# Products with zero weights between the score and sum products of an attention kernel

## The chip, the cores and the metric

The kernel runs on one core of a Trainium2 chip. The metric is the device time of one execution in microseconds (us). A core has a matrix engine (TensorE, PE in the profile, its weight loads PEld), a vector engine (DVE), an engine for exponentials and the like (ACT), a general engine (POOL) and an engine that issues transfers (SP). Each takes its own instructions in order; they wait for each other by semaphores. Matrix products are written to PSUM, which has 8 banks of 512 fp32 columns by 128 partitions.

## The reference, cut to what matters

Four layers, two kinds, on 2048 tokens of 512 features, 32 heads of 16:

```python
x = x + _A_ref(_layernorm(x), A_wq, A_wk, A_wv, A_wo, A_beta)
x = x + _B_ref(_layernorm(x), B_wqkv, B_wo)
x = x + _A_ref(_layernorm(x), A_wq, A_wk, A_wv, A_wo, A_beta)
x = x + _B_ref(_layernorm(x), B_wqkv, B_wo)

def _B_ref(x, wqkv, wo):
    q, k, v = ...
    scores = jnp.einsum('bhqd,bhkd->bhqk', q, k) * Dh ** (-0.5)
    p = _softmax(scores, axis=-1)
    o = jnp.einsum('bhqk,bhkd->bhqd', p, v)
    return (lambda x, *d: x.transpose(*d))(o, 0, 2, 1, 3).reshape(B, S, D) @ wo
```

Kind A attends causally within each of four segments of 512 tokens, and adds a memory that is read with phi(q) and updated with phi(k) and v from segment to segment, mixed by a gate per head. Kind B is plain attention over all 2048 tokens.

## The kernel before, in words

The program is laid out by a planner in Python: it appends operations to one list per engine and derives all waits from the buffers and PSUM banks that they read and write (`Sched.add`). There is no loop on the chip.

The work is cut into *units*. A unit takes three PSUM banks, each with the scores of 128 keys by 512 queries of one head (kind A: 512, 384 + 128 or 256 columns, what the causal mask leaves). Two sets of three banks (0 to 2, 3 to 5) alternate. `unit()` (L970) issues three score products, with 32 rows of features each, `ps<-qm,KB` or `ps<-qm,KA` in the profile, and one ACT instruction that writes the exponentials of all three banks, `pT<-ps` (L1023). In kind B a unit may also hold a fourth score product, into bank 7, whose exponential DVE works out in steps (`dx_chain`, L747). `pv_step()` (L1128), two units later (three in kind A), issues the products of the exponentials with the values, `ps<-pT,VB` or `ps<-pT,VA` (from DVE's exponentials `ps<-dxo,VB`). These are the sums: weights of 128 rows and 17 columns (16 values and a one for the denominator), added up in bank 6, at partition 0, 32, 64 or 96, by `r`, which counts the four strips of 32 feature rows, two heads to a strip. A *group* is four heads, one of each strip, with 512 queries and their keys: 64 banks for a whole group of kind B (some are split over the key segments), 12 for one of kind A. After a group's last sum DVE transposes bank 6 (L1083), and the next group's first sum waits for that.

The main loop, `attention()` (L1154), does for each unit, in this order: scores and exponentials; outside kind A and when enough units lie ahead, background work that uses PE; sums that are due; background work. Background work is a list of tasks in generator form, run by credits for PE and DVE: layer norms, the projections to q, k and v (`proj_fm`, `proj_tm`, L488 and L499: four products of 512 columns by 128 rows, issued two at a time, `ps<-xT,wA`, `ps<-wA,xT` and the same with `wB`), the memory of kind A (`task_mem`) and the output products (`task_out`, L664: four products at once, `ps<-woA,oT` or `ps<-woB,oT`). They all go to bank 7. So PE's queue has, per unit: scores, maybe projections, sums, maybe projections, and then the next scores. Every product goes through `mm` (L324), so all have line L325.

The names that the change touches: `self.cur`, the group whose sums are in progress, or None between groups; `started[0]`, true once the sums of the group's head at partition 0 have begun; `wB`, the projection weights of kind B, loaded once at the start; `self.step`, the number of units begun.

## Time and profile before

| | us |
|---|---|
| median of 3 runs | 2149.47 |
| lowest, highest | 2146.08, 2149.75 |
| the profiled execution | 2149.91 |
| its span, first to last instruction | 2148.0 |
| ACT busy in the span | 2008.6 |
| PE busy in the span | 1789.5 |
| DVE busy in the span | 1593.3 |
| mean granted TensorE clock | 0.694 of full |

PE's busy time counts a product from its start to the modelled end of its last column, with the way through the array; several products of different rows or columns of the array run side by side. The costliest groups of instructions are the exponentials of L1023 (1985.8 us), the scores of kind B (682.5), the sums from ACT's exponentials (664.8) and from DVE's (205.4). Transfers are small: 24.5 MB, and the DMA engines are all but idle after the first fifth.

### The profile page before, as it was taken

To read this page: it belongs to the slowest core of one execution; us is meant where nothing else is said; L and a number is where in the kernel's file an instruction comes from. 1 tells how busy PE (TensorE), PEld (TensorE's weight loads), DVE (VectorE), ACT (ScalarE), POOL (GpSimd) and SP (SyncE) were. 2 spreads that over 40 slices of the span, in tenths; PEclk is the share of its full clock that TensorE was granted. 3 is DMA by queue.
4 is the path that set the end of the run, shared out by engine and by line. 5 is a ranking of instruction groups with operands and counts; after the bars stand their busy time and mean duration, and the time that the engine had idled before them with its cause. 6 is when DMAs were issued, how large, how long until landed. Compare 5 with 4: busy or idle time off the path is not lost.

```text
span 2148.0 us, 30875 instructions
## 1 busy us (share of the span) xinstructions
PE 1789.5 (83%) x11634; PEld 414.1 (19%) x11634; DVE 1593.3 (74%) x2806; ACT 2008.6 (94%) x1618; POOL 407.0 (19%) x832
## 2 busy tenths in 40 slices
PE   7788888888788787787877888888888888888888
PEld 3222222211211212212222112221111111111111
DVE  6655665487658885688857975548799989988996
ACT  5788998999989999899998998889999999999997
POOL 3532433020150002400033102501100000000000
PEclk9889888756957968769866558785655565556555
DMA  4011000000000000000000001000000000000000
GB/s 138 16 25 21 20 14 13 6 1 13 8 1 11 1 13 9 11 11 1 15 11 6 1 3 19 11 11 1 11 1 1 1 11 1 1 1 11 1 1 11
DMA packets 67125, 24.54 MB, mean 11 GB/s; under 512 B 59808, under 2 KB 66464, under 8 KB 66976
## 3 DMA queue, kind: packets, MB, share of 16 engines
q1 hardware_dynamic: 66976, 22.57, 4.6%
q8 instruction: 91, 1.49, 0.3%
q14 instruction: 58, 0.48, 0.1%
HBM read 6.30 MB, written 2.10 MB: 4 GB/s over the span
## 4 chain that ended last, share of the span: by engine, by line
issue 39%; ACT 28%; PE 19%; DVE 9%; POOL 4%; DMA 1%; SPq 0%; POOLq 0%; ACTq 0%; DVEq 0%
ACT pT L1023 27%; PE ps L325 19%; POOL ob L1096 1%; POOL pT L1038 1%; POOL qm L941 1%; DVE tT L1083 1%; DVE VB L341 1%; DVE VA L341 1%; DVE dxt L732 1%; DMA xT<-xn 1%; DVE QB L341 0%; ACT amem L513 0%; DVE x L686 0%; DVE lnst L431 0%; DVE QA L341 0%
## 5 line engine op out<-in xcount | busy, mean ns | idle before, releaser
L1023 ACT ACTIVATE pT<-ps 128x1536 bf16<-128x1536 f32 (+2 forms) x1589 | 1985.8, 1439 | 111.1 <-PE ps L325 97.9
L325 PE MATMUL ps<-qm,KB 32*128 32x512 bf16 x4096 | 682.5, 524 | 235.3 <-ACT pT L1023 217.6
L325 PE MATMUL ps<-pT,VB 128*17 128x512 bf16 x3716 | 664.8, 515 | 23.7 <-DVE tT L1083 18.3
L1096 POOL TENSOR_TENSOR ob<-tT,rd 128x256 bf16<-128x256 f32 x128 | 99.8, 780 | 1207.5 <-DVE rd L1087 1168.3
L732 DVE TENSOR_SCALAR dxt<-ps 128x512 uint32<-128x512 f32 x380 | 261.0, 687 | 86.3 <-PE ps L325 80.3
L325 PEld LDWEIGHTS ps<-qm,KB 32*128 32x128 bf16 x4096 | 133.8, 96 | 762.9 <-ACT pT L1023 679.6
L1038 POOL TENSOR_SCALAR_AFFINE_SELECT pT<-pT 128x256 bf16<-128x256 bf16 (+2 forms) x512 | 210.2, 427 | 322.4 <-ACT pT L1023 313.1
L766 DVE SCALAR_TENSOR_TENSOR dxo<-dxt,dxz 128x1024 int16<-128x1024 uint16 (+1 forms) x203 | 235.1, 1158 | 4.6
L325 PEld LDWEIGHTS ps<-pT,VB 128*17 128x17 bf16 x3716 | 119.1, 90 | 520.3 <-issue 452.9
L325 PE MATMUL ps<-dxo,VB 128*17 128x512 bf16 x380 | 205.4, 541 | 0.4 <-DVE dxo L766 0.4
L325 PE MATMUL ps<-qm,KA 32*128 32x512 bf16 (+3 forms) x1024 | 127.5, 376 | 39.6 <-ACT pT L1023 31.8
L760 DVE TENSOR_TENSOR dxz<-dxz,dxo 128x1024 f16<-128x1024 f16 (+1 forms) x203 | 135.1, 666 | 4.3
L325 PE MATMUL ps<-pT,VA 128*17 128x512 bf16 (+3 forms) x1024 | 121.2, 378 | 18.5 <-DVE tT L1083 10.9
L756 DVE TENSOR_SCALAR dxo<-dxt 128x1024 f16<-128x1024 uint16 (+1 forms) x203 | 132.9, 655 | 2.2 <-PE ps L325 2.0
L764 DVE TENSOR_TENSOR dxz<-dxz,dxo 128x1024 f16<-128x1024 f16 (+1 forms) x203 | 131.8, 649 | 2.1
L1083 DVE STREAM_TRANSPOSE tT<-ps 128x512 f32<-128x512 f32 x112 | 79.7, 712 | 70.6 <-PE ps L325 70.4
L941 POOL TENSOR_SCALAR qm<-QB,par 128x512 bf16<-128x512 bf16 x102 | 81.6, 808 | 180.2 <-PE ps L325 179.9
L758 DVE TENSOR_SCALAR dxz<-dxo 128x1024 f16<-128x1024 f16 (+1 forms) x203 | 88.7, 437 | 6.8
L325 PE MATMUL ps<-xT,wB 128*128 128x512 bf16 x256 | 82.9, 433 | 9.2 <-DMA xT<-xn 2.5
L686 DVE TENSOR_TENSOR x<-x,ps 128x512 bf16<-128x512 bf16 x64 | 44.0, 688 | 60.2 <-PE ps L325 60.0
L762 DVE TENSOR_SCALAR dxz<-dxz 128x1024 f16<-128x1024 f16 (+1 forms) x203 | 83.7, 412 | 6.7
L325 PE MATMUL ps<-xT,wA 128*128 128x512 bf16 x256 | 78.6, 419 | 10.3 <-DVE QA L341 5.3
(89 smaller groups left out, 917.9 us busy)
## 6 DMA issues: line engine op xcount, KB each, us to landing
out_dram<-x SPq DMA_DIRECT2D x8, 256.0 KB, 2.1
x<-in_A_x_dram SPq DMA_DIRECT2D x3, 512.0 KB, 10.9
wB<-in_B_wqkv_dram SPq DMA_DIRECT2D x1, 1536.0 KB, 12.7
xT<-xn SPq DMA_TRANSPOSE x60, 2.5
x<-in_A_x_dram SPq DMA_DIRECT2D x4, 128.0 KB, 2.4
wA<-in_A_wk_dram SPq DMA_DIRECT2D x1, 512.0 KB, 4.4
wA<-in_A_wq_dram SPq DMA_DIRECT2D x1, 512.0 KB, 5.5
wA<-in_A_wv_dram SPq DMA_DIRECT2D x1, 512.0 KB, 6.3
```

Source lines behind the costliest of these rows:

```text
L325: self.sc.add("pe", lambda e: e.matmul(out, lhsT, rhs, start=start, stop=stop, skip_group_check=True), reads=reads, banks=[(bank, "w", all ...
L732: self.op("dve", lambda e: e.tensor_scalar(self.dxt[:, b, i, :], o, SCALE * LOG2E * 65536, 127.0 * 65536, op0=ALU.mult, op1=ALU.add), writ ...
L756: self.op("dve", lambda e: e.tensor_scalar(f, lo, 2.0 ** -16, None, op0=ALU.mult), reads=bt, writes=bo)
L758: self.op("dve", lambda e: e.tensor_scalar(z, f, EXP_C3, EXP_C2, op0=ALU.mult, op1=ALU.add), reads=bo, writes=bz)
L760: self.op("dve", lambda e: e.tensor_tensor(z, z, f, ALU.mult), reads=bo + bz, writes=bz)
L764: self.op("dve", lambda e: e.tensor_tensor(z, z, f, ALU.mult), reads=bo + bz, writes=bz)
L766: self.op("dve", lambda e: e.scalar_tensor_tensor(ob, hi, 128.0, z, op0=ALU.mult, op1=ALU.add), reads=bt + bz, writes=bo)
L941: self.op(eng, (lambda m, q, col: lambda e: e.tensor_scalar(m, q, col, 0.0, op0=ALU.mult, op1=ALU.add))(m, q, col), reads=[bq, self.b_par] ...
L1023: self.sc.add("act", (lambda dst, src: lambda e: e.activation(dst, src, ACT.Exp, scale=SCALE))(dst, src), writes=self.b_pT[slot * 3 + i:sl ...
L1038: self.op("pool", (lambda blk, pat: lambda e: e.affine_select(blk, blk, pattern=pat, compare_op=ALU.is_ge, fill=0.0, base=0, channel_multi ...
L1083: self.op("dve", lambda e: e.transpose(tT.rearrange("p a b -> p (a b)"), src), reads=bsrc, writes=[bt], bank=bk, alloc=al)
L1096: self.op("pool", lambda e: e.tensor_tensor(ob, tT[:, :, 0:16], rb, ALU.mult), reads=[bt, br], writes=[self.b_ob[oi][g.e]])
```

## The change

A function `keep_busy` is called at the end of each unit from the eleventh on. If a group's sums are in progress and have begun at partition 0, it adds products to bank 6 until the unit has 1024 columns of background products. Projections and output products add 512 each to that count (`bg_cols`), the memory's products and the fourth score product don't. The added products have a tile of zeros, 128 rows by 17 columns, as weights and 512 columns of `wB` as moving data, and add to partitions 0 to 16 of the running sums without starting or ending them, so the sums keep their values. A unit without projections gets two, a unit with at least one pair of projections or output products gets none, and a unit between groups gets none.

```diff
+    BUSY_COLS = 1024
...
+        self.zero = sb("zero", [P, 17], bf)
...
+    def keep_busy(self):
+        g = self.cur
+        while g is not None and g.started[0] and self.bg_cols < self.BUSY_COLS:
+            bank = self.banks[6]
+            self.mm(self.ps[0:17, bank.col0:bank.col0 + 512], self.zero[:, :], self.wB[:, 0, 0:512], False, False,
+                    [self.b_zero, self.b_wB[0]], bank, g.acc)
+            self.bg_cols += 512
...
+        pool(lambda e: e.memset(self.zero[:, :], 0.0), [self.b_zero])
...
         for ci in range(NCH):
             if ci == 2:
                 yield ["cont"], 2, 690
+            self.bg_cols += 512
             self.mm(o, w[:, ci, off + c * 128:off + (c + 1) * 128], self.xT[:, slot, ci, :], ci == 0, ci == NCH - 1,
                     [bw] + self.b_xT[slot], bank, al)
...
             for n, (a, c, ba) in enumerate(srcs):
+                self.bg_cols += 512
                 self.mm(o, a[:, ti * 128:(ti + 1) * 128], wo[:, c, :], n == 0, n == len(srcs) - 1, list(ba) + [bwo], bank, al)
...
-        self.step = 0
+        self.step = self.bg_cols = 0
...
             self.run_deferred(False)
             self.background(False if split else None)
+            if self.step > 10:
+                self.keep_busy()
+            self.bg_cols = 0
             n += 1
```

The same line stands in `proj_tm` as in `proj_fm`. `BUSY_COLS` is a constant of the class.

More of the change, by code (lines that the diff above doesn't have):

```diff
@@ L298, in alloc @@
         self.b_dxt = n2("dxt", 2, 2)
-        self.b_dxz = B("dxz")
+        self.b_dxz, self.b_zero = B("dxz"), B("zero")
         self.b_dxo = n1("dxo", self.NDX)
@@ L684, in task_out @@
             for n, (a, c, ba) in enumerate(srcs):
+                self.bg_cols += 512
                 self.mm(o, a[:, ti * 128:(ti + 1) * 128], wo[:, c, :], n == 0, n == len(srcs) - 1, list(ba) + [bwo], bank, al)
```

## The prediction

> **What bounds the kernel now.** I read the page first, for the engines' shares.

> ```profile
> PE 1789.5 (83%) x11634; PEld 414.1 (19%) x11634; DVE 1593.3 (74%) x2806; ACT 2008.6 (94%) x1618; POOL 407.0 (19%) x832
> ...
> ACT  5788998999989999899998998889999999999997
> ...
> PEclk9889888756957968769866558785655565556555
> ```

> ACT does the exponentials and is busy 2008.6 of 2148.0 us. So 139.4 us of ACT idle is all that any change outside ACT can win. In the last quarter ACT's digits are 9 although the TensorE clock is near half. Next, who ACT waits for:

> ```profile
> ACT pT L1023 <- PE ps L325: 97.9, 137, 4.2
> ACT pT L1023 <- POOL pT L1038: 8.4, 16, 1.2
> ACT xT L476 <- PE ps L329: 7.4, 1, 7.4
> ```

> Of it 97.9 us is score products that came late. Then stretches in which the trace's clock record holds one value (it has only 1.0 and 0.5, 826 and 1317 us in all):

> ```profile
> 1304.00:1362.00 58.00, 48.97 (x354) 13.68 (x351) 28.48 (x53) 51.74 (x49) 16.65 (x38) 1.00 0.03 6
> 1758.00:1942.00 184.00, 161.47 (x935) 28.77 (x932) 167.00 (x260) 183.43 (x137) 14.48 (x16) 0.50 0.00 1
> ```

> Columns: length; busy time (instructions) of PE, PEld, DVE, ACT, POOL; clock. At full clock there are 354 products in 58 us, at half 935 in 184 us with ACT idle for 0.57 us only. The clock alone costs nothing while a unit has no projections. Now single units in the timeline: a plain one at half clock, one with two projection products at full clock, and one with four output products at half clock. Columns: start, length, engine, line, what, count.

> ```profile
> 1503.15 0.61 PE L325 MATMUL ps<-qm,KB 32*128 32x512 bf16 x3 [0.20 <-ACT pT L1023]
> 1503.69 0.60 PE L325 MATMUL ps<-pT,VB 128*17 128x512 bf16 x3
> 1504.50 0.61 PE L325 MATMUL ps<-qm,KB 32*128 32x512 bf16 x3 [0.20 <-ACT pT L1023]
> ```

> ```profile
> 177.53 0.39 PE L325 MATMUL ps<-qm,KB 32*128 32x512 bf16 x3
> 177.85 0.60 PE L325 MATMUL ps<-wA,xT 128*128 128x512 bf16 x2
> 178.39 0.39 PE L325 MATMUL ps<-pT,VB 128*17 128x512 bf16 x3
> 178.71 0.39 PE L325 MATMUL ps<-qm,KA 32*128 32x512 bf16 x3
> ```

> ```profile
> 1255.56 0.61 PE L325 MATMUL ps<-qm,KB 32*128 32x512 bf16 x3
> 1256.11 1.89 PE L325 MATMUL ps<-woB,oT 128*128 128x512 bf16 x4
> 1257.92 0.60 PE L325 MATMUL ps<-pT,VB 128*17 128x512 bf16 x3
> 1258.46 0.61 PE L325 MATMUL ps<-qm,KB 32*128 32x512 bf16 x3
> 1259.17 1.45 ACT L1023 ACTIVATE pT<-ps 128x1536 bf16<-128x1536 f32 x1 [1.18 <-PE ps L325]
> ```

> Starts are to be read: the unit of ACT is 1.34 us (1503.15 to 1504.50). At half clock the scores take PE 0.54 us and the sums again 0.54, 1.08 of 1.34. At full clock each takes 0.32 and a pair of projections 0.54: 1.18 in all, which fits. A single product of 512 columns streams 0.22 us at full clock (two end in 0.60, one in 0.39) and 0.43 at half. Four output products at half clock make a unit of 2.90 us (1255.56 to 1258.46); ACT then stands 1.18 us. So the loss lies where projections meet the half clock.

> **What sets the clock.** I cut the timeline into steps of 3.41 us (every stretch of the clock record is a multiple of it) and took, from the starts, the share of each step in which at least one product streams. Of 243 steps at full clock, the 35 with a share under 0.43 were all followed by half clock and the 201 from 0.45 up all by full. Of 385 at half clock, one of the 325 under 0.76 was followed by full, 3 of the 18 from there to 0.80, and 32 of the 42 above. Taken by occupied cells or by the number of products no such edge shows. A plain unit streams 2 x 0.213 of 1.34 us, 0.32, at full clock and falls back; at half clock it streams 0.64 and doesn't rise.

> **The change, part by part.** Setup gains one memset of 17 columns on POOL, beside loads that end later: nothing. The order of all old instructions is unchanged on every engine. PE gains 2092 products in 1046 pairs, after 1046 of the 1492 units (a unit: a run of score products up to the next). 325 units have projections or output products and get none, 121 have no sum in progress and get none. 765 of the pairs follow units that now run at half clock. A pair waits for nothing new: wB was issued at 13.4 us and landed 12.7 us later, the first pair comes at some 51 us. Behind it in PE's queue stand the next unit's scores, for which ACT waits.

> A pair has the sums' shape (128 rows, 17 columns), streams 2 x 0.213 us at full clock, and I charge it 0.43 to 0.54 us by the projection pair. A unit with it is then 1.07 to 1.18 us of PE at full clock, under ACT's 1.34. At half clock it is 1.82 to 1.93 us, over it. It streams 0.64 of 1.34 us at full clock, over the 0.43 edge, so the clock should stay. Where the three sums leave out the first quarter of the columns, the pair's first product can run beside them and the share is 0.48, still over. At half clock it streams 1.71 of 1.93 us, 0.88, over 0.80: the clock should rise within one or two steps. So I expect nearly full clock all along.

> ACT's idle time now, sorted by unit and clock (25.4 us lie before the first unit and can't change):
> - 53 units with projections at half clock: 32.6 us, 0.615 each. At full clock 272 such units have 39.4 us, 0.145 each. Full clock gives 53 x 0.47 = 24.9 us back. Ends: 10 us, if half of it is DVE or transfers late at those places, and all 32.6.
> - 78 units of the first kind of layer (A, narrower exponentials) that get pairs, at half clock: 20.0 us, 0.256 each. Nearest is the A unit with two projections at full clock, 0.184: 5.6 us back. Ends: 0 and 78 x (0.256 - 0.088) = 13, by the 25 such units now at full clock.
> - 942 B units that get pairs: 15.1 us now, 13 ns each in the 686 at half clock. With a pair at full clock PE's load (1.07 to 1.18) is about theirs (1.08). Ends: 13 ns each, 3 us back, and 56 ns, the B unit with four projections at full clock, 38 us lost. I take 20 ns, nearest the first: 4 us lost.
> - Relapses. Where a group ends, a unit has no pair and PE waits for the transpose of bank 6; a step there streams about (0.43 + 1.54 x 0.85)/3.41 = 0.51, with a unit of share 0.48 near 0.45, at the edge. One relapse: about 2 to 2.5 units at 1.82 to 1.93 us, 0.5 to 0.6 over ACT's 1.34 each, less some 0.5 us by which scores are early: 0.9 us. Of 128 group ends I take 9: 8 us. Ends: 0 and one in two, 58 us.

> Sum: -24.9 - 5.6 + 4 + 8 = -18.5 us. Span 2148.0 - 18.5 = 2129.5. Its own execution was 2149.91, 1.9 us beside the span and 0.4 above the median of the three: **2131 us**.

> [...]

> **Rivals.**
> 1. Slower: relapses decide. With 24.9 + 5.6 - 4 = 26.5 us won, 30 relapses at 0.9 us eat it. At one in two group ends: 2149.9 - 26.5 + 58 = 2181 us. For it: pairs turn a harmless half clock into a PE-bound one, and 128 group ends offer the place. Against: PE, when late, has no gaps, and 0.88 is well over the edge.
> 2. Nothing changes (within 0.2%, 4.3 us, what a measurement of this kernel can tell from no change): ACT idles for DVE, transfers and POOL behind PE, or wins equal losses. For it: at full clock the same units still idle 39.4 us. Against: four to 0.615.
> 3. The gate doesn't count products with zero weights, or few columns: the clock stays, and 765 pairs cost 0.59 us each, 451 us: 2600 us. Against: the edge was the same for steps filled by score products, sums or projections.
> 4. More is won: every low end at once, 2149.9 - 32.6 - 13 - 3 = 2101 us, with the rest of the half-clock idle some 2095.

> **How the numbers follow.** Forecast 0.50 (2112 to 2145), rival 4 0.14, rival 2 0.10, rival 1 0.20, rival 3 0.06. Faster by over 0.2% is forecast and rival 4, 0.64; same 0.10; slower 0.26. The range, 2095 to 2165, takes in 4, 2 and rival 1 up to some 45 relapses; what it leaves out is the rest of rival 1 and rival 3.

> **What would show it.** Right: PEclk at 9 in nearly all slices, ACT's wait for PE near 75 us, four-product units of about 1.6 us, ACT still gapless in the last quarter. Wrong: a mean clock under 0.9; many half-clock steps behind group ends with ACT idle there; or ACT idle in B units far over 20 ns at full clock, which would mean that PE's 1.18 of 1.34 leaves too little to catch up.

## The result, and the profile after

The changed kernel takes 2141.78 us (median of 6 runs, 2139.26 to 2142.92) against 2149.68 us, a ratio of 0.9963 (95% interval 0.9953 to 0.9974): faster by 0.37%, where 0.9% was forecast. The profiled execution took 2140.73 us with a span of 2138.6. Page of the changed kernel (all lines of `mm` are now L337, the exponentials L1039):

```profile
PE 1797.9 (84%) x13626; PEld 497.4 (23%) x13726; DVE 1591.0 (74%) x2806; ACT 2007.1 (94%) x1618; POOL 404.8 (19%) x833
...
ACT  5689998999989999899998999999999999999997
...
PEclk9899999999999999899988999999999999999999
...
L337 PE MATMUL ps<-wB,zero 128*17 128x512 bf16 x2092 | 642.8, 390 | 0.0
```

The clock row is the great change: 9 nearly everywhere, a mean of 0.966 after 0.694. PE has 2092 more products and about the same busy time (a hundred of the old products have no record in this trace, hence x13626). But ACT's idle time is 131.5 us after 139.4. ACT's waits and the late stretch of steady units, the same units as 1758 to 1942 us of before (columns as there):

```profile
ACT pT L1039 <- PE ps L337: 88.3, 130, 3.8
```

```profile
1750.00:1934.00 184.00, 153.39 (x1191) 39.11 (x1187) 166.88 (x260) 182.93 (x137) 14.42 (x16) 0.98 0.00 1
```

ACT waits for scores 88.3 us, not the 75 that I named as the sign of being right. The late stretch went from clock 0.50 to 0.98 and ACT did the same 137 exponentials in it. Next, the timeline of a plain unit with its pair, and of a unit with four output products of the same task as the one that the prediction shows:

```profile
1765.55 0.39 PE L337 MATMUL ps<-qm,KB 32*128 32x512 bf16 x3 [0.20 <-ACT pT L1039]
1765.87 0.39 PE L337 MATMUL ps<-pT,VB 128*17 128x512 bf16 x3
...
1766.10 0.59 PE L337 MATMUL ps<-wB,zero 128*17 128x512 bf16 x2
...
1766.89 0.40 PE L337 MATMUL ps<-qm,KB 32*128 32x512 bf16 x4 [0.20 <-ACT pT L1039]
```

```profile
1256.48 0.39 PE L337 MATMUL ps<-qm,KB 32*128 32x512 bf16 x3
1257.01 1.04 PE L337 MATMUL ps<-woB,oT 128*128 128x512 bf16 x4
1257.98 0.39 PE L337 MATMUL ps<-pT,VB 128*17 128x512 bf16 x3
...
1258.30 0.39 PE L337 MATMUL ps<-qm,KB 32*128 32x512 bf16 x3
```

The pair fits under ACT's 1.34 us: PE then still waits 0.20 us for ACT. The unit with four products takes 1.82 us (1256.48 to 1258.30) instead of 2.90; some 1.6 was named as the sign of being right.

**Where the time went.** Both programs have the same 1492 units in the same order, so ACT's idle time can be compared unit by unit (us, from the two traces):

| units | before | after |
|---|---|---|
| B, projections or output products (213) | 29.3 | 17.1 |
| B, with a pair (943) | 15.6 | 11.2 |
| A, projections or output products (112) | 42.6 | 40.6 |
| A, with a pair, no memory products (79) | 17.5 | 21.5 |
| A, with a pair and memory products (24) | 4.7 | 13.3 |
| all others | 4.2 | 2.9 |

B units won 17 us and A units lost 10, so 7.5 us of idle time went in the units. The rest of the 9.4 us of span is 1.4 us of ACT's own time and 0.4 us at the start. What a pair does in an A unit with memory products, timeline before and after:

```profile
1114.41 0.60 PE L325 MATMUL ps<-pT,VA 128*17 128x512 bf16 x3 [0.34 <-POOL pT L1038]
1114.95 0.61 PE L325 MATMUL ps<-Mn,phq 128*128 128x128 bf16 x4
1115.49 0.61 PE L325 MATMUL ps<-qm,KA 32*128 32x512 bf16 x3
...
1116.21 2.79 ACT L1023 ACTIVATE pT<-ps 128x1536 bf16<-128x1536 f32 x2 [0.70 <-PE ps L325]
```

```profile
1113.07 0.60 PE L337 MATMUL ps<-pT,VA 128*17 128x512 bf16 x3 [0.66 <-DVE tT L1099]
1113.60 0.61 PE L337 MATMUL ps<-Mn,phq 128*128 128x128 bf16 x4
1114.14 1.02 PE L337 MATMUL ps<-wB,zero 128*17 128x512 bf16 x2
1115.10 0.61 PE L337 MATMUL ps<-qm,KA 32*128 32x512 bf16 x3
...
1115.81 3.02 ACT L1039 ACTIVATE pT<-ps 128x1536 bf16<-128x1536 f32 x2 [1.95 <-PE ps L337]
```

The four memory products were already in the unit and PE was late. The pair stands between them and the scores, at half clock 0.96 us (1114.14 to 1115.10), and ACT's wait grows from 0.70 to 1.95 us. Four units later in the changed kernel the clock is full, and again four memory products and a pair stand before the scores:

```profile
1120.01 0.60 PE L337 MATMUL ps<-wB,zero 128*17 128x512 bf16 x2
...
1120.55 0.39 PE L337 MATMUL ps<-qm,KA 32*128 32x512 bf16 x3
...
1121.05 1.45 ACT L1039 ACTIVATE pT<-ps 128x1536 bf16<-128x1536 f32 x1 [0.32 <-PE ps L337]
```

Here the pair takes 0.54 us (1120.01 to 1120.55) and ACT waits 0.32; PE had also waited less ahead of it, 0.19 us for the transpose where it was 0.66. So it matters at which clock the pair runs. The mean of 0.966 hides that of the 27 falls of the clock in this trace 20 lie in A units. Of the 103 pairs after A units 32 still ran at half clock; ACT's idle time in those units grew from 12.5 us before to 25.8. In the 71 units whose pair ran at full clock it shrank from 9.7 to 8.9. With memory products and a pair at full clock, 13 units, it grew by 0.6 us in all. The whole loss in A units with pairs is thus in those where the clock had fallen, with memory products (11 units, 8.0 us) or without (21 units, 5.4 us).

### The profile page after: what moved, and what is told of

Its sections match the earlier page's. It is cut to its first block, busy times and chain, and to the rows that moved or that the text cites. A ratio compares the mean times of both kernels' runs of the same rounds, so it can differ in the third digit from the quotient of the medians.

```text
span 2138.6 us, 34960 instructions
## 1 busy us (share of the span) xinstructions
PE 1797.9 (84%) x13626; PEld 497.4 (23%) x13726; DVE 1591.0 (74%) x2806; ACT 2007.1 (94%) x1618; POOL 404.8 (19%) x833
## 4 chain that ended last, share of the span: by engine, by line
issue 38%; ACT 26%; PE 14%; DVE 6%; POOL 4%; DMA 0%; SPq 0%; POOLq 0%; ACTq 0%; DVEq 0%
ACT pT L1039 25%; PE ps L337 14%; POOL ob L1112 2%; POOL pT L1054 1%; POOL qm L957 1%; DVE tT L1099 1%; DVE dxt L748 1%; DVE VB L353 1%; DVE dxo L782 0%; DVE KB L353 0%; DVE x L702 0%; DVE QB L353 0%; DVE VA L353 0%; ACT amem L528 0%; DMA xT<-xn 0%
## 5 line engine op out<-in xcount | busy, mean ns | idle before, releaser
L1039 ACT ACTIVATE pT<-ps 128x1536 bf16<-128x1536 f32 (+2 forms) x1589 | 1984.9, 1547 | 103.6 <-PE ps L337 88.3
L337 PE MATMUL ps<-qm,KB 32*128 32x512 bf16 x4096 | 509.9, 387 | 206.6 <-ACT pT L1039 188.9
L337 PE MATMUL ps<-wB,zero 128*17 128x512 bf16 x2092 | 642.8, 390 | 0.0
L337 PE MATMUL ps<-pT,VB 128*17 128x512 bf16 x3716 | 496.8, 386 | 20.7 <-DVE tT L1099 15.3
L337 PEld LDWEIGHTS ps<-qm,KB 32*128 32x128 bf16 x4096 | 126.8, 91 | 750.5 <-ACT pT L1039 653.0
L337 PEld LDWEIGHTS ps<-wB,zero 128*17 128x17 bf16 x2092 | 179.5, 92 | 115.1 <-issue 7.7
L337 PEld LDWEIGHTS ps<-pT,VB 128*17 128x17 bf16 x3716 | 115.5, 87 | 349.2 <-issue 298.4
L337 PE MATMUL ps<-dxo,VB 128*17 128x512 bf16 x380 | 146.6, 386 | 0.1
L337 PE MATMUL ps<-qm,KA 32*128 32x512 bf16 (+3 forms) x1024 | 109.3, 330 | 33.3 <-ACT pT L1039 25.3
L337 PE MATMUL ps<-pT,VA 128*17 128x512 bf16 (+3 forms) x1024 | 106.0, 334 | 22.0 <-DVE tT L1099 14.2
```

The lines of the kernel that those rows point to most:

```text
L337: self.sc.add("pe", lambda e: e.matmul(out, lhsT, rhs, start=start, stop=stop, skip_group_check=True), reads=reads, banks=[(bank, "w", all ...
L1039: self.sc.add("act", (lambda dst, src: lambda e: e.activation(dst, src, ACT.Exp, scale=SCALE))(dst, src), writes=self.b_pT[slot * 3 + i:sl ...
```

## The experiments

Each kernel was timed against the kernel before on the same chip. "Pairs" are the two products with zero weights.

**Only B, only A.** The unit's kind decides:

```diff
-            if self.step > 10:
+            if self.step > 10 and not isA:
```

> Pairs only after units of kind B (943 of the 1046). Theory 1, that the pairs win in the B units and lose in the A units: between the two traces ACT's idle time fell by 17 us in B units (46.0 to 28.9) and rose by 10 us in A units (67.9 to 77.6); without the A pairs the first stays and the second goes, so about 2133 us, 0.992 of before. Rival, that the loss in A units is a slower clock left behind by something else and the A pairs help: no better than the change, 2140 us or more.

Measured: 2139.59 us, ratio 0.9961 (0.9948 to 0.9973). Better than before, but not by the 17 us of the idle times, and not told apart from the change. Its A units are back at 68.5 us of idle time, as in before; its B units have 38.2, not 28.9. The timeline of this kernel shows where they lost:

```profile
2029.64 0.39 PE L337 MATMUL ps<-qm,KB 32*128 32x512 bf16 x3 [0.63 <-ACT pT L1039]
2030.63 0.61 PE L337 MATMUL ps<-pT,VB 128*17 128x512 bf16 x4 [0.59 <-DVE tT L1099]
2031.02 1.06 PE L337 MATMUL ps<-wB,zero 128*17 128x512 bf16 x2
2032.01 0.61 PE L337 MATMUL ps<-qm,KB 32*128 32x512 bf16 x3
...
2032.73 1.45 ACT L1039 ACTIVATE pT<-ps 128x1536 bf16<-128x1536 f32 x1 [0.45 <-PE ps L337]
...
2033.93 0.61 PE L337 MATMUL ps<-qm,KB 32*128 32x512 bf16 x3
```

This is the relapse of the prediction: at a group's end the sums wait for the transpose, the products go from 0.39 to 0.61 us (half clock), and the next unit with a pair takes 1.92 us (2032.01 to 2033.93), so that ACT waits 0.45 us and in the next unit 0.47 again.

> Pairs only after units of kind A (103). Theory 1: the loss alone, about 10 us over before, 2159 us, 1.0045. Rival: the A pairs cost nothing by themselves, 2147 to 2152 us.

Measured: 2157.87 us, 1.0037 (1.0025 to 1.0049). The A pairs alone lose 8 us, as the theory had it. The split by clock is that of the change: in its trace 34 of the pairs ran at half clock, with 12.9 us of ACT's idle time in those units before and 27.3 now; in the other 69 units it went from 9.3 to 8.4.

**Memory products counted.** One line ahead of each of the three products in `task_mem`, so that 36 units get no pair:

```diff
+                    self.bg_cols += 512
                     self.mm(self.ps[:, o:o + 128], self.phq[:, c, ti * 128:(ti + 1) * 128], self.Mn[:, c, :, :], True, True,
```

> The memory's products are counted as background products, so 36 units with them get no pair (1010 pairs). Theory 1 in its narrow form, that the loss is in units which already hold memory products (ACT idle 4.7 to 13.3 us in them): about 2134 us, 0.9925. Rival, that any pair in an A unit loses: only 2 to 4 us better than the change, 2138 to 2140 us.

Measured: 2132.07 us (2124.02 to 2141.02), 0.9926 (0.9903 to 0.9948). The time is that of the narrow form: leaving out 36 of 1046 pairs gives about as much again as the whole change. The spread is wide, and a later run shows that the memory products are not the whole of it.

**One product instead of two** (`BUSY_COLS = 512`).

> One product instead of two after the same 1046 units. By the edge read from the steps of 3.41 us (0.43 to stay at full clock, 0.80 to rise) a unit then streams 0.48 of 1.34 us at full clock, 0.32 where the product runs beside the sums; the mean is at the edge. Theory, that the clock follows the streamed share: a mean clock between 0.75 and 0.95, half of PE's extra load, 2134 to 2142 us. Rival, that any regular product holds the clock: clock 0.96 and 2135 us or less; rival, that two are needed: clock 0.70 and 2147 to 2152 us.

Measured: 2147.52 us, 0.9998 (0.9986 to 1.001), with a mean clock of 0.911. The clock followed the theory, the time didn't. In its trace B units have 36.8 us of idle time (46.1 before), A units 74.5 (67.9), and after the first 300 units the clock fell 36 times in B units, with some 10 to 13 us of ACT's idle time around these falls, depending on how many units are counted to each. A clock of 0.91 that keeps falling was worth nothing here.

**A units without memory products alone, B units without them alone.** Both from the kernel with the memory counted, with `and isA` or `and not isA`:

> Pairs only after the 79 units of kind A without memory products. All 103 A pairs alone cost 8 us (ratio 1.0037), and ACT's idle time grew by 8.4 us in the 24 with memory products. Theory: the memory units carry the whole loss, so this comes out within 2 us of before, 2147 to 2151 us. Rival, that any pair in an A unit loses (idle in the 79 grew by 5 us there): 2153 us or more.

Measured: 2156.63 us (2150.0 to 2163.51), 1.0022 (1.0009 to 1.0035). The theory falls: by themselves these 79 pairs lose some 5 us too. Idle time in the 79 units went from 17.5 to 22.3 us. All of that growth is in the 31 units whose pair ran at half clock (10.6 to 16.5 us); in the other 48 it fell from 6.9 to 5.8.

> Pairs only after the 931 units of kind B without memory products. With all B pairs it was 2139.6, with these and the 79 A pairs 2132.1. Theory: the 79 A pairs help once the B pairs hold the clock up to them, so without them 2138 to 2141 us. Rival, that the 12 pairs in B units with memory products made the difference: 2131 to 2134 us.

Measured: 2132.92 us, 0.9912 (0.9897 to 0.9927). Without any A pair the time can't be told from that of the kernel with them (0.9926), so here the 79 pairs neither win nor lose clearly. The difference from the run with all 943 B pairs (0.9961) is not explained by its 12 further pairs: the units that have them hold 0.7 us of idle time there and 0.5 us here. In that run's trace more relapses fell into B units (8 with 6.2 us against 7 with 3.6) and single A units had up to 1.75 us more. I leave it open.

**Four products instead of two**, where a unit has no background products:

```diff
             if self.step > 10:
+                if not self.bg_cols:
+                    self.bg_cols = -1024
                 self.keep_busy()
```

> Four products instead of two, after the 1010 units without projections and memory products; measures the load of a product. At 0.216 us for each streamed product at full clock a B unit takes PE 0.64 + 4 x 0.216 = 1.50 us against ACT's 1.34. Theory, that PE then bounds: 931 x 0.16 = 150 us over the 2132 us of the pairs, about 2280 us, mean clock over 0.95. Rival, that products with 17 columns run beside the sums and scores: under 2200 us.

Measured: 2300.96 us, 1.0691 (1.0673 to 1.0709), clock 0.986. The timeline of this kernel:

```profile
1765.67 0.39 PE L337 MATMUL ps<-qm,KB 32*128 32x512 bf16 x3
...
1766.22 1.03 PE L337 MATMUL ps<-wB,zero 128*17 128x512 bf16 x4
1767.18 0.39 PE L337 MATMUL ps<-qm,KB 32*128 32x512 bf16 x4
```

A unit takes 1.51 us (1765.67 to 1767.18), and no row of PE has a wait: PE bounds, as the theory had it. So each product costs 0.22 us of PE (four take 1.03 us in this row, two 0.59 in that of the changed kernel), two fit under 1.34 us and four don't.

**No pairs in the last layer** (`and self.cur.L < 3`), from the kernel with the memory counted.

> Pairs as with memory products counted, but none in the last layer (500 of the 1010 units). Theory: full clock is worth something only where projections, output products or the memory stand beside the units; in the last layer before the change ACT idles 3 to 5 us in such units, so 2135 to 2138 us with a mean clock near 0.8. Rival, that every unit gains with the clock: half the gain gone, 2140 us or more.

Measured: 2143.63 us (2135.5 to 2145.18), 0.9951 (0.9935 to 0.9968), clock 0.805. The median is over the theory's 2138 us, but against the kernel before, on the same chip, the ratio lost is 0.0025 (0.9926 to 0.9951), some 5 us, and the two intervals overlap: the run doesn't decide. A later one takes this up.

**The strip that the pair adds to.** From the B pairs without memory products; `strips` holds the strips of the unit's sums in order:

```diff
+            r = next((x for x in self.strips[::-1] if g.started[x]), 0)
-            self.mm(self.ps[0:17, bank.col0:bank.col0 + 512], ...
+            self.mm(self.ps[32 * r:32 * r + 17, bank.col0:bank.col0 + 512], ...
```

> As the 931 B pairs, but the pair adds to the strip of the unit's last sum (partition 0, 32, 64 or 96), so it can't run beside the sums: a unit then always streams 0.64 of 1.34 us at full clock and a step with a group's end 0.51, both over the edge of 0.42 to 0.45. Theory, that the clock falls by the streamed share: at most 3 falls in B units after the first 300 units (7 with partition 0), 2128 to 2133 us, ratio 0.989 to 0.992. Rival, that falls come from waits of PE at group ends whatever the pair does: as many falls, 2133 us.

Measured: 2127.86 us (2127.81 to 2130.42), 0.9905 (0.9892 to 0.9918). After the first 300 units the clock did not fall in B units, but for one fall at 1375.6 us, where kind A passes into kind B. The median is the lowest of all kernels, but the ratio can't be told from the 0.9912 of the same pairs at partition 0: the falls are shown by the traces, the gain in time isn't. Its late stretch, with columns as above, has no idle time of ACT left:

```profile
1745.00:1925.00 180.00, 153.44 (x1175) 40.52 (x1171) 164.22 (x257) 180.00 (x135) 14.48 (x16) 1.00 0.00 1
```

With a strip that none of the unit's sums uses (`x not in self.strips`):

> The opposite: the pair adds to a strip that none of the unit's sums uses, so its first product runs beside them. A unit streams 0.64 us of 1.34, 0.48, and a step with a group's end (0.43 + 1.54 x 0.64)/3.41 = 0.41. Theory: the clock falls at most group ends, 25 or more falls in B units after the first 300 units, each 0.3 to 0.6 us of ACT idle: 2140 to 2148 us, mean clock 0.80 to 0.90. Rival, that PE's smaller load (0.86 instead of 1.08 us) is worth more than the clock: 2128 to 2133 us.

Measured: 2128.74 us, 0.9911 (0.9898 to 0.9924), clock 0.94, 8 falls. The expectation fails. In its trace 389 of the 931 units with a pair have four sums or more, mostly one from DVE's exponentials, and can leave no strip free. Of the pairs in B units at full clock after the first 300 units, 481 started beside the sums and 362 behind them; in the kernel with partition 0, 132 and 715; with the strip of the last sum, 3 and 854. So the run made its case in part. It had 8 falls where partition 0 had 7, so the falls did not grow much with the pairs that run beside the sums, and the time doesn't tell the strips apart.

The strip of the last sum after A and B units:

> The strip of the last sum, after A and B units without memory products (1010 pairs). Theory: as the 1010 pairs with partition 0 (2132 us), less the B falls: 2127 to 2132 us; the 79 A pairs win in the projections beside them about what they lose, so within 3 us of the B pairs alone. Rival: the A pairs cost 5 us, as they do alone: 2134 us or more.

Measured: 2138.44 us (2134.32 to 2145.47), 0.9958 (0.9943 to 0.9973). The rival holds: by the ratios (0.9905 and 0.9958) the 79 A pairs here cost some 11 us beside the B pairs. In its trace the 25 units whose pair ran at half clock went from 11.7 to 16.9 us of idle time, the other 54 from 5.8 to 6.9. Over the runs they win nothing or lose.

**The last layer again**, from the kernel with the lowest time:

> As the B pairs on the strip of the last sum (2127.9 us), but none in the last layer (422 pairs). ACT's idle time in the last 492 units was 3.7 us before the change and 0.1 us with those pairs, the time that they took 678.5 and 671.3 us. Theory by idle time: 3.6 us lost, 2130 to 2133 us. Rival by elapsed time, that a gap also costs ACT's own overlap between two instructions: 7 to 8 us lost, 2134 to 2137 us.

Measured: 2139.81 us, 0.9951 (0.9935 to 0.9967), clock 0.78. Between the ratios lie 0.0046, some 10 us, nearer the rival and over it. In the traces the starts of the last 492 exponentials lie 7.3 us in all over 1.342 us each here (5.3 us of it gaps), 0.4 us with the pairs and 5.8 us in before (3.7 gaps). From the last exponential's start to the end it takes 13.3 us here and 11.1 with the pairs. That makes 9.2 us, the 10 of the ratios. At the seven gaps of before, 3.7 us long, the starts came 6.1 us late in all; so a gap there cost more than its length, and why is not shown. Of this kernel's 5.3 us of gaps 4.7 stand at units with output products and in the unit behind each. The pairs in the steady units win nothing there, but they hold the clock for those: with them it was 1.00 in the late stretch shown above, without them the mean was 0.78.

## Why the prediction was right and wrong

- **The clock** came out at 0.966, nearly full as forecast, and the edges stood, less sharply. In the changed kernel's trace, of the 3.41 us steps at full clock 21 of the 22 with a streamed share under 0.40 were followed by half clock, 5 of 21 from there to 0.45, and 1 of some 540 above. Of those at half clock all 22 from 0.80 up were followed by full, 5 of 12 from 0.72 to 0.80, none of 8 below. But "nearly full clock all along" was wrong for the A units: 32 of their 103 pairs ran at half clock. With products of zero weights and 17 columns the late stretch stood at 0.98 where it had 0.50, so rival 3, by which such products don't count, is out.
- **The pair's price** of 0.43 to 0.54 us at full clock: 0.44, as 0.22 for each product in the run with four; from the pair to the next scores 0.54 in the timeline shown above. At half clock 0.96 there. The 0.213 that the forecast takes for one product is half of the 0.427 us between two starts at half clock (24 pairs of the changed trace at 0.426 to 0.427); at full clock the two products of a pair start 0.215 to 0.216 us apart in 826 of them.
- **"942 B units ... 4 us lost"**: 4 us were won (15.6 to 11.2), relapses included. **"Relapses: 8 us"**: 6 in B units after the first 300, one of them behind the last exponential, with 3.7 us, some 0.7 each where 0.9 was named. Rival 1, that relapses eat the gain, came true in part, in the A units that the next points take up.
- **"53 units with projections at half clock ... 24.9 us back"** was mis-sized: 13.5 us (32.6 to 19.1). The 30 B units gave 11.3 of their 14.2, more than I took. The 23 A units gave 2.2 of their 18.4. Three of them, with 3.1 us, come before the eleventh unit, where no pair can be. Five more, with 4.4 us, stand at one place where PE waited ahead of them, which no pair changes. The timeline of the changed kernel shows the place (for the units elsewhere the cause is not shown):

```profile
324.38 0.39 PE L337 MATMUL ps<-pT,VA 128*17 128x512 bf16 x4 [1.67 <-DVE tT L1099]
...
327.82 0.63 PE L337 MATMUL ps<-xT,wB 128*128 128x512 bf16 x1 [1.26 <-DMA xT<-xn]
328.38 0.61 PE L337 MATMUL ps<-qm,KA 32*128 32x384 bf16 x6
...
329.10 1.45 ACT L1039 ACTIVATE pT<-ps 128x1536 bf16<-128x1536 f32 x1 [1.52 <-PE ps L337]
```

  PE stands 1.67 us for a transpose and 1.26 us for a transfer, and its queue can't bring the pair forward. I had given all 53 units the full-clock average; the low end of 10 us, for just this, was nearer.
- **"78 units of kind A ... 5.6 us back"** is the step that failed, with its sign: 11.1 us were lost in them (20.0 to 31.1), 7.1 of it in the 21 with memory products. I had priced all of them by a row at full clock, the A unit with two projections. But in 30 of the 78 the pair still ran at half clock, and these went from 11.6 to 23.4 us; the 48 that did come to full clock went from 8.4 to 7.6. At half clock a pair puts 0.96 us before scores that are already late, and most where memory products stand in the unit as well, which I had said are not counted without asking what stands in such a unit. Relapses I had priced at the ends of groups by the B unit alone. The low end, 0, excluded a loss. The runs with A pairs alone split the same way by clock, which speaks for this account. But the 30 had more idle time of ACT already before (0.39 us each, against 0.18 in the 48), and no run held the clock full in the A units, so how much is the pair's and how much the place's stays open.

The 25 A units with pairs that were at full clock already lost another 1.5 us (2.2 to 3.7), the units not named here won 2.0. So 7.4 us of idle time went, where the sum had 18.5: 11.4 too much on the projections, 18.2 on the A pairs, and 16.4 too little on the B pairs and relapses. That the time still lies within the forecast's 2112 to 2145 us is partly luck: two errors one way were more than halved by one the other way. The run with the memory counted, 16 us faster than before, and the one with B pairs alone and no memory units, 19 us, come near the forecast by leaving out what it had mis-sized.

## What to carry to other kernels

Work added to hold TensorE's clock paid here where products crowd a unit (11.3 us in the 30 B units with projections) and cost where the clock fell all the same and the queue was already late (11.6 to 23.4 us in 30 A units), so sort its price by the clock at which it will run, and count everything that the unit holds, the small products too. Work out the share that streams in each step of the clock record, at the ends of groups too; in the B units' traces a pair that could not run beside the sums left one of the falls, at 1375.6 us, where there had been 7, though the time did not show it. A clock at full speed was worth nothing in units in which nobody waits for PE (137 exponentials in 184 us at a clock of 0.50 and at 0.98): look for those in which someone does, and for what holds the clock up to them.
